# w_out's float64 tiles, from the third on, loaded as two halves into the buffers of the partial results

## The chip, the cores and the metric

One core of one Trainium2 chip. The metric is device time in microseconds (us) of one execution; three executions of the kernel before are shown, and the median is what the prediction is set against.

## What is computed

Three stages in a row, in the precision of float32 results. The weights of the two feed-forward stages are float64; q, k, v and omega are float32.

```python
q_p, k_p = phi(q / D**0.25), phi(k / D**0.25)      # exp(x @ omega.T - |x|^2/2 - max) / sqrt(m)
kv = einsum('bhsm,bhsd->bhmd', k_p, v); z = sum(k_p, axis=2)
x = einsum('bhsm,bhmd->bhsd', q_p, kv) / (einsum('bhsm,bhm->bhs', q_p, z)[..., None] + 1e-06)
x = x.transpose(0, 2, 1, 3).reshape(2304, 512)
y = ((x @ w_a) * (x @ w_b)) @ w_out                # w_a, w_b: 512 x 1536, w_out: 1536 x 512
h = maximum(y @ w_in2, 0); out = (h * h) @ w_out2  # 512 x 2048, 2048 x 512
```

## The kernel before, in words

The change lies in the middle stage, `y = ((x @ w_a) * (x @ w_b)) @ w_out`, which runs interleaved with the attention that makes its `x`.

**Passes.** The hidden width 1536 is cut into 12 tiles f of 128 columns, the 2304 tokens into 9 blocks of 256. `PASSES` (L770) takes block 0 with f = 0 to 5, block 1 with f = 0 to 5, block 0 with f = 6 to 11, block 1 with f = 6 to 11, block 2 in the same two halves, and then pairs of blocks with all f. For each f, `a_units` (L775) issues 24 matmuls "ab" (12 for w_a, 12 for w_b), then, two f later (`LAG`), the 12 matmuls "y" of `outs` (L802), which accumulate over f in the PSUM banks y0 and y1. Every product is three matmuls over a high and a low part of each operand (`TERMS`).

**Weights.** The weights come as float64, 8 bytes a word. `load` (L183) brings them raw into a tile `raw` of [128, 2, 512, 2] int32 (8 KB a partition; the pool has two of them, "the pairs' places"). One `raw` holds either a pair, the tile f of w_a and of w_b (2 x 512 KB), or one tile f of w_out (512 KB, half of the place). `split` (L200) turns the words into float32 high and low parts: ACT scales the upper words (L211), DVE puts sign, exponent and mantissa together in three operations on `p` (L212, L216, L220; the last one reads `raw` and so frees it), ACT casts the high part (L226), DVE subtracts to get the low part (L227). The pairs stay in `W` for good; a tile of w_out goes into one of three `wo` buffers and is stored to `wo_d` (L1603), from which the later passes load it again (L1597). `load_split` (L250) lets at most two loaded tiles wait for their split. Below, o6 to o11 are the tiles f = 6 to 11 of w_out, first needed in the third pass.

**Partial results.** `ypool` has two buffers of [128, 2, 256] float32 (2 KB a partition), tag "ys". They hold `V2` of the attention at the start; `y_s`, the scaled result at the end of a first-half pass, which is stored to `y_d` (L845 to L847); `y_p`, that result loaded again for the second half (`prefetch`, L971), to which DVE adds the new half (L840) and from which it is stored; and, from the seventh pass on, `tz`, weight sums (L889).

**Order.** The code is written in one order, but a scheduler of the Tile framework, with costs of its own, decides how the instructions stand on each engine; each engine and each queue then runs strictly in that order. All loads and stores named here are issued by SP, one after the other: one that waits holds all behind it.

Of the kernel before, what the change touches and what calls it, by code (L numbers as in the profile page):

```python
# [44 lines left out]
def kernel(  # L45
# [13 lines left out]
    nc = tc.nc  # L59
# [121 lines left out]


    def load(*parts):  # L183


        raw = top["raw"].tile([128, 2, 512, 2], I32, tag="raw", name="raw")
        for x, (w, f, rows) in enumerate(parts):
# [12 lines left out]
    def split(raw, t, behind=None, apart=False, put_off=None):  # L200

        n = raw.shape[1]
        a_, p_ = (
            top["cut"].tile([128, 2, 512], F32, tag=x, name=x)[:, 0:n] for x in "ap"
        )
        for x in (slice(0, 1), slice(1, 2)) if apart else (slice(0, n),):
            a, p, r, o = a_[:, x], p_[:, x], raw[:, x], t[:, x]
            with tc.issue_after(behind.ins) if behind else nullcontext():  # L210
                nc.scalar.activation(out=a, in_=f32(r[:, :, :, 1]), func=ACTF.Copy, scale=WORD_SCALE)  # L211
            nc.vector.tensor_scalar(  # L212
# [6 lines left out]
            )  # L219
            nc.vector.scalar_tensor_tensor(  # L220
                out=p.bitcast(U32), in0=r[:, :, :, 0].bitcast(U32), scalar=29,
                in1=p.bitcast(U32), op0=ALU.logical_shift_right, op1=ALU.bitwise_or,
            )

# [550 lines left out]
    def a_units():  # L775
# [26 lines left out]
        def outs(pi, f):  # L802
# [26 lines left out]
            if wide:  # L829
                for c in range(KC):  # L830
                    t = ypool.tile([128, 2, N], F32, tag="ys", name="y_s")
                    nc.scalar.mul(out=t, in_=yp[pi][c], mul=Y_SCALE)
                    for x, i in enumerate(bl):
                        nc.sync.dma_start(out=y_cols(i)[:, c, :], in_=t[:, x, :])
                return
            i = bl[0]
            for c in range(0, KC, 2):
                if f0:
                    t = part[pi, c]
                    nc.vector.scalar_tensor_tensor(  # L840
                        out=t, in0=yp[pi][c // 2], scalar=Y_SCALE, in1=t,
                        op0=ALU.mult, op1=ALU.add,
                    )
                else:
                    t = ypool.tile([128, 2, N], F32, tag="ys", name="y_s")  # L845
                    nc.scalar.mul(out=t, in_=yp[pi][c // 2], mul=Y_SCALE)
# [124 lines left out]
        def prefetch(pi, f):  # L971
            bl, f0, f1 = PASSES[pi]
            if f0 and f == f1 - 1:
                for c in range(0, KC, 2):
                    part[pi, c] = ypool.tile([128, 2, N], F32, tag="ys", name="y_p")
                    nc.sync.dma_start(out=part[pi, c], in_=y_cols(bl[0])[:, c:c + 2, :])
# [813 lines left out]
```

## Time and profile before

| | us |
|---|---|
| three executions | 976.73, 978.43, 978.84 (median 978.43) |
| the profiled execution | 979.28 |
| its span, first to last instruction | 977.2 |
| TensorE (PE) busy | 961.5 (98%) |
| VectorE (DVE) busy | 728.8 (75%) |
| ScalarE (ACT) busy | 551.5 (56%) |
| mean granted TensorE clock | 0.999 of full |

The profile is of one execution. PE is TensorE's matmuls, PEld its weight loads, SPq the queue of loads and stores. A busy share is an average over the whole span; the stages named above lie in its first 310 us, and the third pass (block 0, f = 6 to 11) from about 124 to 174 us.

### The profile page before, as it was taken

To read this page: it belongs to the slowest core of one execution; us is meant where nothing else is said; L and a number is where in the kernel's file an instruction comes from. 1 tells how busy PE (TensorE), PEld (TensorE's weight loads), DVE (VectorE), ACT (ScalarE), POOL (GpSimd) and SP (SyncE) were. 2 spreads that over 40 slices of the span, in tenths; PEclk is the share of its full clock that TensorE was granted. 3 is DMA by queue.
4 is the path that set the end of the run, shared out by engine and by line. 5 is a ranking of instruction groups with operands and counts; after the bars stand their busy time and mean duration, and the time that the engine had idled before them with its cause. 6 is when DMAs were issued, how large, how long until landed. Compare 5 with 4: busy or idle time off the path is not lost.

```text
span 977.2 us, 18208 instructions
## 1 busy us (share of the span) xinstructions
PE 961.5 (98%) x6625; PEld 898.0 (92%) x6625; DVE 728.8 (75%) x1688; ACT 551.5 (56%) x1310; POOL 28.8 (3%) x54
## 2 busy tenths in 40 slices
PE   7999999999999999999999999999999999999998
PEld 6799998999998889889998888899999999999998
DVE  3888689887787865565456989789787347988794
ACT  5876566666655643253433544677676565555561
POOL 4000100000000000000000000000000000000000
PEclk9999999999999999999999999999999999999999
DMA  8656976655775365346547989246666869944301
GB/s 207 208 176 204 307 234 212 226 179 182 218 213 167 130 199 171 113 153 188 170 143 254 350 304 339 66 160 207 216 227 220 317 250 357 390 135 146 115 17 50
DMA packets 121961, 198.39 MB, mean 203 GB/s; under 512 B 28944, under 2 KB 84752, under 8 KB 119440
## 3 DMA queue, kind: packets, MB, share of 16 engines
q1 hardware_dynamic: 120336, 195.65, 60.5%
q0 software_dynamic: 1536, 1.58, 0.6%
q8 instruction: 53, 0.87, 0.4%
q14 instruction: 36, 0.29, 0.1%
HBM read 136.90 MB, written 60.29 MB: 202 GB/s over the span
## 4 chain that ended last, share of the span: by engine, by line
PE 81%; DVE 7%; DMA 5%; ACT 4%; issue 2%; SPq 0%; DVEq 0%; ACTq 0%
PE y L811 13%; PE abw L786 9%; PE oY L1478 8%; PE pY L1294 7%; PE ab L786 7%; PE oX L1478 5%; PE oW L1478 5%; PE sP L919 5%; PE pW L1294 4%; PE sR L919 3%; PE ps_n L638 3%; PE ps_kv L571 3%; PE ps_p L415 3%; PE ps_p L490 2%; DMA raw<-in_moe_w_b_dram 2%; PE ps_qt L628 2%
## 5 line engine op out<-in xcount | busy, mean ns | idle before, releaser
L786 PE MATMUL abw<-x_all,W 128*128 128x512 f32 x432 | 104.1, 392 | 0.0
L786 PEld LDWEIGHTS abw<-x_all,W 128*128 128x128 f32 x432 | 80.0, 188 | 15.7
L786 PE MATMUL ab<-x_all,W 128*128 128x256 f32 x576 | 84.9, 290 | 0.4 <-ACT W L226 0.4
L786 PEld LDWEIGHTS ab<-x_all,W 128*128 128x128 f32 x576 | 74.0, 189 | 1.7 <-ACT W L226 0.6
L811 PE MATMUL y<-g_mid,wo 128*128 128x512 f32 x288 | 75.1, 401 | 0.0
L811 PE MATMUL y<-gs,wo 128*128 128x256 f32 x432 | 66.5, 290 | 0.0
L811 PEld LDWEIGHTS y<-g_mid,wo 128*128 128x128 f32 x288 | 51.9, 188 | 10.1
L811 PEld LDWEIGHTS y<-gs,wo 128*128 128x128 f32 x432 | 56.6, 189 | 1.0 <-DVE wo L227 0.2
L1294 PE MATMUL pY<-W,M 128*128 128x384 f32 x228 | 44.1, 336 | 0.4 <-ACT F L1312 0.4
L499 ACT COPY c<-ps_p 128x256 f32<-128x256 f32 x76 | 27.7, 372 | 28.6 <-PE ps_p L490 28.1
L501 DVE CUSTOM_DVE_ANT_0 c<-ps_p,c 128x128 f32<-128x128 f32 x152 | 38.2, 285 | 7.5 <-ACT c L499 6.8
L786 PE MATMUL ab<-x,W 128*128 128x256 f32 x288 | 42.5, 288 | 0.0
L1442 ACT CAST W<-F 128x384 fp32r<-128x384 f32 x57 | 29.1, 513 | 22.9 <-PE oX L1478 11.0
L1478 PE MATMUL oX<-W 128*128 128x256 f32 x351 | 41.9, 276 | 0.0
L1478 PEld LDWEIGHTS oX<-W 128*128 128x128 f32 x351 | 40.8, 188 | 0.0
L1294 PEld LDWEIGHTS pY<-W,M 128*128 128x128 f32 x228 | 39.8, 188 | 1.0 <-ACT F L1312 0.9
L1320 ACT ACTIVATE F<-F 128x384 f32<-128x384 f32 x48 | 24.7, 518 | 26.9 <-DVE F L1315 26.7
L1478 PE MATMUL oY<-W 128*128 128x256 f32 x315 | 38.6, 277 | 0.0
L786 PEld LDWEIGHTS ab<-x,W 128*128 128x128 f32 x288 | 37.6, 191 | 0.1
L506 ACT ACTIVATE qp<-c,nm 128x128 f32<-128x128 f32 x88 | 31.0, 397 | 11.3 <-DVE nm L501 10.8
L1478 PEld LDWEIGHTS oY<-W 128*128 128x128 f32 x315 | 37.1, 188 | 0.0
L419 DVE TENSOR_REDUCE nm<-ps_p 128x4 f32<-128x512 f32 (+1 forms) x44 | 24.7, 564 | 14.9 <-PE ps_p L415 14.7
(287 smaller groups left out, 2408.7 us busy)
## 6 DMA issues: line engine op xcount, KB each, us to landing
wo<-wo_d SPq DMA_DIRECT2D x60, 512.0 KB, 3.9
s_d<-F SPq DMA_DIRECT2D x24, 768.0 KB, 4.7
tsum<-t_d SPq DMA_DIRECT2D x26, 512.0 KB, 4.0
t_d<-cut SPq DMA_DIRECT2D x40, 256.0 KB, 2.9
raw<-in_moe_w_out_dram SPq DMA_DIRECT2D x32, 256.0 KB, 5.2
raw<-in_moe_w_in_dram SPq DMA_DIRECT2D x16, 512.0 KB, 6.4
raw<-in_moe_w_a_dram SPq DMA_DIRECT2D x12, 512.0 KB, 3.8
raw<-in_moe_w_b_dram SPq DMA_DIRECT2D x12, 512.0 KB, 5.8
```

Source lines behind the costliest of these rows:

```text
L415: state["proj"] = nc.tensor.matmul(ps[:, 2 * x:2 * x + 2].rearrange("p h m -> p (h m)"), lhsT=s, rhs=OMZ.rearrange("p h m -> p (h m)"), st ...
L499: nc.scalar.copy(out=c, in_=ps[:, :, 1, :])
L501: nc.vector.tensor_tensor_reduce(out=c[:, x, :], in0=ps[:, x, 0, :], in1=c[:, x, :], scale=1.0, scalar=3.0e38, op0=ALU.add, op1=ALU.min, a ...
L506: nc.scalar.activation(out=dst[:, 2 * n + x, :], in_=c[:, x, :], func=ACTF.Exp, scale=-1.0, bias=nm[:, x:x + 1],)
L571: lambda h=h, j=j: nc.tensor.matmul(ps[:, h, :], lhsT=kp[:, 4 * h + j, :], rhs=V2[h][:, j] if odd else V[:, j, h, :], start=(j == j0), sto ...
L638: lambda x=x: nc.tensor.matmul(pn[:, x, :], lhsT=t["qT"][:, x % 2 * len(g) + x // 2, :], rhs=kv[:, x % 2, :], start=True, stop=True,)
L786: nc.tensor.matmul(ps, lhsT=wv[:, s_, kc, :], rhs=x[..., kc, m_, :], start=(kc == 0 and (s_, m_) == TERMS[0]), stop=(kc == KC - 1 and (s_, ...
L811: nc.tensor.matmul(y_part(pi, f, c), lhsT=wo[pi, f][:, s_, c * 128:(c + 1) * 128], rhs=g[:, m_, :],  start=(f == f0 and (wide or c % 2 == ...
L919: nc.tensor.matmul(ps[:, z], lhsT=b(z, s_, kk), rhs=a[:, kk, m_, :], start=(first and z == 0 and kk == 0 and (s_, m_) == TERMS[0]), stop=( ...
L1294: nc.tensor.matmul(ps[c][:, x, 0:TH], lhsT=w[:, s_, 128 * kk:128 * kk + 128], rhs=y[:, ai, kk, m_, :], start=((c, x) not in seen and kk == ...
L1442: ahead_of["cast"] = nc.scalar.copy(out=sop[:, 0], in_=src)
L1478: nc.tensor.matmul(tiles_of(p, t), lhsT=sops[n][:, s_, 128 * t:128 * t + 128], rhs=w[:, m_, :], start=(fresh and k == 0 and (t % 2 == 0 or ...
```

## The change

The tiles of w_out with f >= 2 no longer go into `raw`. Each is loaded as two halves of 512 int32 columns (256 KB, 2 KB a partition) into two buffers of `ypool`. `split` then reads the halves apart: two ACT operations in place of one for the upper words, two DVE operations in place of one for the last step on `p`; the other steps stay whole. `y_stage` allocates the partial results' buffers, and first has all waiting w_out tiles of that kind split.

```diff
--- before.py
+++ after.py
@@ -180,9 +180,27 @@
 
 
 
+    O_APART = 2
+
+    def y_stage(name):
+
+        while any(x[1][0] == "o" and x[1][1] >= O_APART for x in waiting):
+            split_next()
+        return ypool.tile([128, 2, N], F32, tag="ys", name=name)
+
     def load(*parts):
 
 
+        if parts[0][2] and parts[0][1] >= O_APART:
+            w, f, _ = parts[0]
+            raws = []
+            for z in range(2):
+                t = ypool.tile([128, 2, N], F32, tag="ys", name="rawo").rearrange("p a n -> p (a n)")
+                nc.sync.dma_start(
+                    out=i32(t), in_=w[f * 128:(f + 1) * 128, 512 * z:512 * z + 512]
+                )
+                raws.append(i32(t).rearrange("p (f w) -> p f w", w=2))
+            return raws
         raw = top["raw"].tile([128, 2, 512, 2], I32, tag="raw", name="raw")
         for x, (w, f, rows) in enumerate(parts):
             t = raw[:, x]
@@ -201,14 +219,24 @@
 
 
 
-        n = raw.shape[1]
+        halves = None
+        if isinstance(raw, list):
+            halves = [(slice(256 * z, 256 * z + 256), r) for z, r in enumerate(raw)]
+        n = 1 if halves else raw.shape[1]
         a_, p_ = (
             top["cut"].tile([128, 2, 512], F32, tag=x, name=x)[:, 0:n] for x in "ap"
         )
         for x in (slice(0, 1), slice(1, 2)) if apart else (slice(0, n),):
-            a, p, r, o = a_[:, x], p_[:, x], raw[:, x], t[:, x]
+            a, p, o = a_[:, x], p_[:, x], t[:, x]
+            if halves:
+                pieces = [(a[:, 0, c], p[:, 0, c], r) for c, r in halves]
+            else:
+                pieces = [(a, p, raw[:, x])]
             with tc.issue_after(behind.ins) if behind else nullcontext():
-                nc.scalar.activation(out=a, in_=f32(r[:, :, :, 1]), func=ACTF.Copy, scale=WORD_SCALE)
+                for a_x, _, r in pieces:
+                    nc.scalar.activation(
+                        out=a_x, in_=f32(r[..., 1]), func=ACTF.Copy, scale=WORD_SCALE
+                    )
             nc.vector.tensor_scalar(
                 out=i32(p), in0=i32(a), scalar1=3, scalar2=0x7FFFFFF8,
                 op0=ALU.logical_shift_left, op1=ALU.bitwise_and,
@@ -217,10 +245,11 @@
                 out=i32(p), in0=i32(a), scalar=-0x80000000, in1=i32(p),
                 op0=ALU.bitwise_and, op1=ALU.bitwise_or,
             )
-            nc.vector.scalar_tensor_tensor(
-                out=p.bitcast(U32), in0=r[:, :, :, 0].bitcast(U32), scalar=29,
-                in1=p.bitcast(U32), op0=ALU.logical_shift_right, op1=ALU.bitwise_or,
-            )
+            for _, p_x, r in pieces:
+                nc.vector.scalar_tensor_tensor(
+                    out=p_x.bitcast(U32), in0=r[..., 0].bitcast(U32), scalar=29,
+                    in1=p_x.bitcast(U32), op0=ALU.logical_shift_right, op1=ALU.bitwise_or,
+                )
 
             def parts(o=o, p=p):
                 state["cast"] = nc.scalar.copy(out=o[:, :, 0, :], in_=p)
@@ -828,7 +857,7 @@
                 return
             if wide:
                 for c in range(KC):
-                    t = ypool.tile([128, 2, N], F32, tag="ys", name="y_s")
+                    t = y_stage("y_s")
                     nc.scalar.mul(out=t, in_=yp[pi][c], mul=Y_SCALE)
                     for x, i in enumerate(bl):
                         nc.sync.dma_start(out=y_cols(i)[:, c, :], in_=t[:, x, :])
@@ -842,7 +871,7 @@
                         op0=ALU.mult, op1=ALU.add,
                     )
                 else:
-                    t = ypool.tile([128, 2, N], F32, tag="ys", name="y_s")
+                    t = y_stage("y_s")
                     nc.scalar.mul(out=t, in_=yp[pi][c // 2], mul=Y_SCALE)
                 nc.sync.dma_start(out=y_cols(i)[:, c:c + 2, :], in_=t)
 
@@ -972,7 +1001,7 @@
             bl, f0, f1 = PASSES[pi]
             if f0 and f == f1 - 1:
                 for c in range(0, KC, 2):
-                    part[pi, c] = ypool.tile([128, 2, N], F32, tag="ys", name="y_p")
+                    part[pi, c] = y_stage("y_p")
                     nc.sync.dma_start(out=part[pi, c], in_=y_cols(bl[0])[:, c:c + 2, :])
 
         t_now = {}
```

The numbers of matmuls, of casts and of stores stay; ten loads, ten ACT and ten DVE operations are added. Since the scheduler goes by other load times, it also sets the instructions anew: PE's order is another one between its 184th and its 1713th matmul of 6271, and the same again from there on. Three pieces follow, as the built programs have them; changed line numbers are those of the changed file, which are 29 higher from L226 on.

The first is from SP's queue, at the end of the second pass. `raw` and `rawo` are loads of float64 words, `wo_d` are stores of finished tiles of w_out (92 is o6), `y_s` the partial result. Before:

```order
L190 DMA raw<-in_moe_w_out_dram 128x1024
L441 DMA qn<-in_q_dram 128x2x64
L194 DMA raw<-in_moe_w_a_dram 128x4x256
L1603 DMA wo_d_92<-wo 128x1024
L194 DMA raw<-in_moe_w_b_dram 128x4x256
L847 DMA y_d_103<-y_s 128x2x256 x2
L1603 DMA wo_d_93<-wo 128x1024
L190 DMA raw<-in_moe_w_out_dram 128x1024
L976 DMA y_p<-y_d_103 128x2x256 x2
L194 DMA raw<-in_moe_w_a_dram 128x4x256
L194 DMA raw<-in_moe_w_b_dram 128x4x256
```

and now:

```order
L212 DMA raw<-in_moe_w_a_dram 128x4x256
L212 DMA raw<-in_moe_w_b_dram 128x4x256
L470 DMA qn<-in_q_dram 128x2x64
L199 DMA rawo<-in_moe_w_out_dram 128x512 x2
L1632 DMA wo_d_92<-wo 128x1024
L470 DMA qn<-in_q_dram 128x2x128
L876 DMA y_d_103<-y_s 128x2x256
L1632 DMA wo_d_93<-wo 128x1024
L876 DMA y_d_103<-y_s 128x2x256
L199 DMA rawo<-in_moe_w_out_dram 128x512
L470 DMA qn<-in_q_dram 128x2x128
L199 DMA rawo<-in_moe_w_out_dram 128x512 x3
```

The last pair (f = 11) stood behind the load of o8 and stands now ahead of that of o7; the loads of y_p are gone from here, and those of o8 stand behind the stores of y_s, whose buffers they take.

The second is from SP's queue, at the end of the third pass (`wo<-wo_d_92` loads o6 again for the fourth). Before:

```order
L190 DMA raw<-in_moe_w_out_dram 128x1024
L1603 DMA wo_d_95<-wo 128x1024
L441 DMA kn<-in_k_dram 128x2x256
L1603 DMA wo_d_96<-wo 128x1024
L1597 DMA wo<-wo_d_92 128x1024
L1603 DMA wo_d_97<-wo 128x1024
L1597 DMA wo<-wo_d_93 128x1024
L847 DMA y_d_103<-y_p 128x2x256 x2
```

and now:

```order
L199 DMA rawo<-in_moe_w_out_dram 128x512 x2
L1632 DMA wo_d_96<-wo 128x1024
L1005 DMA y_p<-y_d_103 128x2x256 x2
L1626 DMA wo<-wo_d_92 128x1024
L1632 DMA wo_d_97<-wo 128x1024
L1626 DMA wo<-wo_d_93 128x1024
L876 DMA y_d_103<-y_p 128x2x256 x2
```

The loads of y_p now stand behind the load of o11, whose buffers they take, and ahead of the first load for the fourth pass.

The third is from PE, at the end of the third pass (y_1895 and y_1896, now y_1921 and y_1922) and the begin of the fourth's sums (y_2496, now y_2536). Before:

```order
L786 MATMUL ab<-x_all,W 128x256 x13
L490 MATMUL ps_p<-OM,S 128x256 x2
L786 MATMUL ab<-x_all,W 128x256
L811 MATMUL y_1895<-gs,wo 128x256 x2
L811 MATMUL y_1896<-gs,wo 128x256 x2
L786 MATMUL ab<-x_all,W 128x256
L811 MATMUL y_1895<-gs,wo 128x256 x4
L811 MATMUL y_1896<-gs,wo 128x256 x4
L628 MATMUL ps_qt<-ident,qp 128x128 x4
L786 MATMUL ab<-x_all,W 128x256 x10
L811 MATMUL y_2496<-gs,wo 128x256 x6
```

and now:

```order
L815 MATMUL ab<-x_all,W 128x256 x18
L840 MATMUL y_1921<-gs,wo 128x256 x2
L840 MATMUL y_1922<-gs,wo 128x256 x2
L444 MATMUL ps_p<-OMZ,T 128x256
L840 MATMUL y_1921<-gs,wo 128x256 x3
L680 MATMUL ps_x<-ident,xh 128x128 x2
L840 MATMUL y_1921<-gs,wo 128x256
L840 MATMUL y_1922<-gs,wo 128x256 x4
L519 MATMUL ps_p<-OM,S 128x256 x2
L815 MATMUL ab<-x_all,W 128x256 x5
L494 MATMUL ps_t_2482<-ident,qn 128x128 x2
L815 MATMUL ab<-x_all,W 128x256 x5
L840 MATMUL y_2536<-gs,wo 128x256 x6
```

The y matmuls of o11 begin as the 1060th matmul of the order and began as the 1026th; those of the fourth pass begin as the 1089th, not the 1053rd, 15 after the last of o11. Those of o9 begin as the 955th (before: 953rd), and from the 1166th on the fourth pass stands where it stood.

## Rows read from the trace of the kernel before

**Rows 1.** The page, busy time: engine, us (share of the span), instructions.
```profile
PE 961.5 (98%) x6625; PEld 898.0 (92%) x6625; DVE 728.8 (75%) x1688; ACT 551.5 (56%) x1310; POOL 28.8 (3%) x54
```

**Rows 2.** Who PE waited for, 113 to 310 us: us in total, times, longest us.
```profile
PE ps_qt L628 <- ACT qp L506: 0.7, 1, 0.7
PE ps_qt L628 <- DVE nm L501: 0.7, 1, 0.7
PE ps_nt L694 <- ACT qT L690: 0.4, 2, 0.2
PE ab L786 <- ACT W L226: 0.4, 1, 0.4
PE ps_qt L628 <- ACT qp L421: 0.3, 1, 0.3
PE ps_xt L706 <- DVE xh L613: 0.2, 1, 0.2
```

**Rows 3.** Who SP's queue waited for, whole span: us in total, times, longest us.
```profile
SPq L190 <- DVE p L220: 27.0, 9, 5.7
...
SPq L194 <- DVE p L220: 18.6, 9, 4.5
```

**Rows 4.** Busy time of each engine (instructions), clock, DMA share, GB/s, 155 to 180 us.
```profile
155.00:180.00 25.00, 24.13 (x193) 22.68 (x193) 23.51 (x70) 15.89 (x41) 1.04 (x2) 1.00 0.65 211
```

**Rows 5.** Groups of DVE, then ACT, by shape, 113 to 180 us: busy us, mean ns.
```profile
L220 DVE SCALAR_TENSOR_TENSOR p<-raw,p 128x512 uint32<-128x512 uint32 x8 | 5.5, 686 | 0.1
...
L1064 DVE TENSOR_TENSOR a_s<-ab,a_s 128x256 f32<-128x256 f32 x11 | 4.6, 420 | 1.0 <-ACT a_s L1063 1.0
...
L211 ACT ACTIVATE a<-raw 128x512 f32<-128x512 f32 x8 | 5.4, 676 | 4.8 <-DVE den L609 1.6 <-DMA raw<-in_moe_w_b_dram 1.4 <-DVE den L612 1.0
...
L1063 ACT ACTIVATE a_s<-ab 128x256 f32<-128x256 f32 x11 | 4.1, 382 | 6.5 <-PE ab L786 6.5
```

**Rows 6.** DMA issues, 113 to 180 us: KB each, median us from issue to landing.
```profile
raw<-in_moe_w_out_dram SPq DMA_DIRECT2D x6, 512.0 KB, 3.8
...
raw<-in_moe_w_a_dram SPq DMA_DIRECT2D x3, 512.0 KB, 3.6
...
y_d<-y_s SPq DMA_DIRECT2D x2, 256.0 KB, 6.3
y_p<-y_d SPq DMA_DIRECT2D x2, 256.0 KB, 3.9
```

**Rows 7.** SP's queue in order of time: start us, us to issue, what.
```profile
137.17 1.44 SPq L847 DMA_DIRECT2D y_d<-y_s  x2
...
143.69 0.93 SPq L976 DMA_DIRECT2D y_p<-y_d  x2
...
161.87 0.33 SPq L190 DMA_DIRECT2D raw<-in_moe_w_out_dram  x1
...
168.97 0.37 SPq L1597 DMA_DIRECT2D wo<-wo_d  x1
```

**Rows 8.** PE in order of time, third pass: start us, us, what [idle before].
```profile
159.52 2.84 PE L786 MATMUL ab<-x_all,W 128*128 128x256 f32 x22
...
162.51 0.74 PE L811 MATMUL y<-gs,wo 128*128 128x256 f32 x4
...
172.22 0.66 PE L811 MATMUL y<-gs,wo 128*128 128x256 f32 x4
...
175.52 0.87 PE L811 MATMUL y<-gs,wo 128*128 128x256 f32 x6
```

**Rows 9.** ACT in order of time: the split of o11.
```profile
165.45 0.67 ACT L211 ACTIVATE a<-raw 128x512 f32<-128x512 f32 x1
...
171.46 0.62 ACT L226 CAST wo<-p 128x512 fp32r<-128x512 f32 x1 [0.20 <-DVE p L220]
```

**Rows 10.** DVE in order of time: the split of o11, then the sum.
```profile
170.74 0.69 DVE L220 SCALAR_TENSOR_TENSOR p<-raw,p 128x512 uint32<-128x512 uint32 x1
...
173.64 1.29 DVE L840 SCALAR_TENSOR_TENSOR y_p<-y,y_p 128x512 f32<-128x512 f32 x2
```

## The prediction, as put on record before the run

> **What bounds the kernel now.** I read the page's busy times first: PE is busy 98% of the span [rows 1]. A change that adds no matmul and takes none away can therefore gain only what PE waits. The change reorders PE's work from its 184th to its 1713th matmul and no further, so I asked next for whom PE waited in that part: from 113 to 310 us it is 2.7 us in all (0.7 + 0.7 + 0.4 + 0.4 + 0.3 + 0.2), and of these only 0.4 us is a wait for the weights, the cast W at L226; the rest are transposes and small products of the attention that wait for ACT or DVE [rows 2]. SP's queue, asked for its own waits, shows what the change goes for: loads of w_out stood 27.0 us in total, and loads of pairs 18.6 us, until DVE had read a raw place [rows 3]. So the places are short, but nearly all of that shortage is hidden: PE had other matmuls in its order. Last, the stretch from 155 to 180 us: DVE is busy 23.51 of 25 us, ACT 15.89, PE 24.13 [rows 4]. There DVE, not the loads, is the engine with least room, and there the last four tiles of w_out are split.
>
> About 0.2%, here 2 us, is what a measurement of this kernel can tell from no change. All waits of rows 2 together are little more than that.
>
> **The change, part by part.** Removed: the turns that pairs and w_out's tiles take at the two raw places. In the first order piece the last pair (f = 11) moves from behind the load of o8 to ahead of that of o7. That pair is the one whose cast PE waits for at about 157.7 us. Gain taken: 0.4 us, that one wait [rows 2]. Bounds: nothing, if DVE is as late with the pair's low part as the load was; 1.3 us, if the waits of the attention in the same stretch (0.4 + 0.3 + 0.2) go too because ACT and DVE are less held up in front of a load.
>
> Added on DVE and ACT: ten times two half operations in place of one. A DVE operation of 256 columns takes 0.420 us, the whole step of 512 takes 0.686 us, so a split costs 2 x 0.420 - 0.686 = 0.15 us, ten of them 1.5 us; on ACT it is 2 x 0.382 - 0.676 = 0.09 us, ten of them 0.9 us [rows 5]. (The 256-column rows are of other operations on float32, the nearest shown.) ACT's share is hidden: it is free for 9 us of the 25 us of the fullest stretch [rows 4]. On DVE four of the ten lie between 155 and 180 us, 4 x 0.15 = 0.6 us, with 1.5 us of room. Taken: +0.3 us, half; bounds 0 and +0.6.
>
> Added on SP: ten more issues of 0.33 us or so [rows 7], 3.3 us spread over 110 us; SP spends far more than that waiting [rows 3], and that wait is the cover. Where SP does not wait for a free place but for a landing, there is no cover: that is the next point.
>
> A half brings half the bytes, but no earlier landing is counted: y_p, 256 KB, lands 3.9 us after issue, w_out, 512 KB, 3.8 [rows 6]. The pieces don't matter either in these rows: w_a comes in pieces of 1 KB (256 words of 4 bytes, L195) and lands in 3.6 us, w_out in rows of 4 KB [rows 6]. The Trainium skill (Perfetto Trace Analysis, DMA Optimizations) speaks against the halves: small transfers, under 2 KB, carry much overhead each, and going from 2 to 4 or 8 KB can help throughput much; these halves go from 4 KB a partition to 2. By that rule each half would land later than the whole did, and the slower rival below would be the likelier; the 1 KB pieces of w_a show no such loss, so I keep 3.9 us.
>
> **The wait that the change adds.** The two buffers of the partial results now hold one tile of w_out at a time. Four tiles in a row (o8 to o11) and then y_p pass through the same two buffers, each load behind the last read of the one before. What one turn takes at least: landing 3.9, second issue 0.3, an ACT half 0.38, the three DVE steps 0.42 + 0.69 + 2 x 0.42 = 1.95; together 6.5 us [rows 5, 6, 7]. Before, with two raw places, the next load ran beside the split: o11 was issued at 161.87 us and its split began on ACT at 165.45 [rows 7, 9]. What PE's order allows for a turn: between the first y of o9 and the first y of o11 there stood 73 matmuls, in 172.22 - 162.51 = 9.71 us, 0.133 each [rows 8]; now 105 stand there, so 14.0 us for two turns, 7.0 each. So a turn fits with half a microsecond to spare, if the split is done at once. It was not always: o11's split took from 165.45 to the start of its last step at 170.74, 5.3 us where the operations alone need 1.8 (0.67 + 0.42 + 0.69), because both engines work in order [rows 5, 9, 10]. Lower bound of the cost: 0. Upper: two turns each late by 6.5 + 3.5 - 7.0 = 3.0 us, 6 us. Taken: 0, since before, too, o11's cast ended at 172.08 and its y began at 172.22 without a wait [rows 8, 9], that is, PE's order had been made to meet the splits closely and it held.
>
> Then y_p. Before, it was loaded at 143.69 us and used at 173.64, 30 us later [rows 7, 10]; a late one cost nothing. Now its loads stand behind the last reads of o11 (second order piece). From the end of o11's last step: y_p lands after 0.4 + 3.9 = 4.3 us [rows 6, 7], the first of two sums of 0.64 us (1.29 for both) is done at 5.0 [rows 10]. PE needs the bank that this sum frees for the first y of the fourth pass. From the same point PE begins the y of o11 after the cast, 0.6 to 0.7 us [rows 9], and reaches the fourth pass's y 29 matmuls later (1060th to 1089th, third order piece), 29 x 0.13 = 3.8 us, at 4.5 us. So 0.5 us of PE time is missing; +0.5 us, with 0 (if o11 is split ahead of its y) and 2 us (a landing like y_s's 6.3 [rows 6]) as bounds. Queued behind y_p on SP is the load of o6 for the fourth pass, which goes out as late; before it went at 168.97 us for a y at 175.52 [rows 7, 8], 6.5 us ahead, so it has some 2 us in hand over a landing.
>
> The partial result's own stores (y_s, 6.3 us to landing [rows 6], issued at 137.17 [rows 7]) now hold up the load of o8, to about 144 us; before, y_p's loads waited there just so, until 143.69. No cost is taken, as o8's y stands 12 matmuls later than it did.
>
> After the 1713th matmul the order is the old one, and what comes after 310 us moves as a block.
>
> Sum: -0.4 + 0.3 + 0 + 0.5 = +0.4 us. The profiled execution, 979.28 us, would become 979.7; it stands 0.85 us over the median of the runs, 978.43, and against that median the forecast is 978.8 us.
>
> **The rivals.** *Slower: the turns at the two buffers set the pace.* The place is the third pass, o9 to y_p; it decides as soon as a turn takes more than 7.0 us. For it: DVE has 1.5 us of room in 25 [rows 4], and o11's split took 3.5 us over its bare operations. Against: the order met the splits within 0.2 us before. Price: o10 and o11 each late by 1 to 1.5 us and y_p's 0.5 to 2 on top: +2.5 to +5, less the 0.4 gained: 980.5 to 983.0 us. Chance 0.3. *Faster: the pairs' earlier loads free the small engines.* ACT stood 1.4 us before loads of pairs in its 512-column operations alone, between 113 and 180 us [rows 5], and the attention's products wait on ACT and DVE [rows 2]. If that clears three quarters or more of the 2.7 us of rows 2, and the turns keep up: 975.7 to 976.4 us. For it is that the waits at 18.6 us of SP's queue fall on pairs [rows 3]; against it that the two longest waits, 0.7 each, lie after the third pass and have to do with no load of weights. Chance 0.2. *No change to speak of because nothing that mattered was moved:* the pairs land earlier and PE's order still has the same matmuls, so 978.0 to 979.0 us; it lies within the forecast's case.
>
> **How the numbers follow.** Forecast's case (within 2 us of 978.4, its own range 977.0 to 980.3) 0.5, slower 0.3, faster 0.2; these are the three chances as well. The range takes all of the forecast's case, the slower one up to 982.4 and the upper part of the faster one from 976.1: 976.1 to 982.4.
>
> **What would show it.** Right: PE's wait for W at L226 is gone; SP's waits of w_out's loads are no shorter, those of pairs are; y_p is issued past 170 us and its sum on DVE waits for a DMA; a y of the fourth pass, or its weight load, begins with a wait of about 0.5 us for that sum. Wrong towards slower: PE idle before y for wo (L255, L256) at o10 or o11, summing to 2 us or more. Wrong towards faster: rows 2's waits mostly gone, with y_p landed before the y of o11 ends.

## The result, and the profile after

The changed kernel takes 984.78 us (median of 6 executions, 982.59 to 986.43); the kernel before, beside it, 978.19 (6 executions, 975.95 to 979.28). Ratio 1.0071, 95% interval 1.0054 to 1.0087: 6.6 us slower, outside the range that was given. The profiled execution has a span of 983.6 us, against 977.2.

The page, busy time (as [rows 1]):

```profile
PE 963.7 (98%) x6625; PEld 897.2 (91%) x6625; DVE 729.9 (74%) x1698; ACT 553.9 (56%) x1320; POOL 29.0 (3%) x54
```

PE's busy time rose by 2.2 us with the same number of matmuls, so most of the loss is idle time. Who PE waited for, 113 to 317 us (us in total, times, longest; as [rows 2]):

```profile
PE y L840 <- DMA wo<-wo_d: 1.2, 1, 1.2
PE ps_xt L735 <- DVE xh L642: 0.9, 1, 0.9
PE ps_qt L657 <- DVE nm L530: 0.7, 1, 0.7
PE ps_p L444 <- ACT T L434: 0.6, 1, 0.6
PE ps_nt L723 <- ACT qT L719: 0.4, 1, 0.4
PE ps_p L519 <- DVE x_all L689: 0.4, 1, 0.4
```

The wait for the cast W is gone. In its place stands one of 1.2 us for a reload of w_out's tile o6, and more waits of the attention's small products for DVE and ACT than before. What SP's queue waited for (as [rows 3]):

```profile
SPq L199 <- DVE p L249: 26.7, 8, 5.3
...
SPq L212 <- DVE p L249: 22.6, 7, 7.1
```

w_out's loads wait as long for a place as they did (27.0 us), the pairs' longer (18.6 before). The stretch from 155 to 180 us (as [rows 4]):

```profile
155.00:180.00 25.00, 23.25 (x181) 21.37 (x180) 21.53 (x64) 14.09 (x39) 0.00 (x0) 1.00 0.43 152
```

DVE, called there the engine with least room, is less busy than before (23.51), and the DMA engines' share fell from 0.65 to 0.43: of w_out's tiles each is now loaded only when the one before is split, as the next rows show.

**The turns.** SP's queue in order of time (start, us to issue, what), third pass:

```profile
144.81 0.34 SPq L199 DMA_DIRECT2D rawo<-in_moe_w_out_dram  x1
...
163.38 0.80 SPq L199 DMA_DIRECT2D rawo<-in_moe_w_out_dram  x2
...
170.93 0.81 SPq L199 DMA_DIRECT2D rawo<-in_moe_w_out_dram  x2
...
177.34 0.89 SPq L1005 DMA_DIRECT2D y_p<-y_d  x2
178.32 0.43 SPq L1626 DMA_DIRECT2D wo<-wo_d  x1
```

These are the first half of o8, then o10, o11, y_p, and the reload of o6. DVE in order of time shows what frees the places:

```profile
157.04 1.22 DVE L249 SCALAR_TENSOR_TENSOR p<-raw,p 128x1024 uint32<-128x1024 uint32 x1
158.18 0.28 DVE L642 TENSOR_TENSOR xh<-ps_nt,den 64x128 f32<-64x128 f32 x1
...
159.72 1.23 DVE L256 TENSOR_TENSOR W<-p,W 128x1024 fp32r<-128x1024 f32 x1 [0.56 <-ACT W L255]
...
162.88 0.76 DVE L249 SCALAR_TENSOR_TENSOR p<-rawo,p 128x256 uint32<-128x256 uint32 x2
...
170.44 0.76 DVE L249 SCALAR_TENSOR_TENSOR p<-rawo,p 128x256 uint32<-128x256 uint32 x2
...
176.85 0.76 DVE L249 SCALAR_TENSOR_TENSOR p<-rawo,p 128x256 uint32<-128x256 uint32 x2
```

The last reads of o9, o10 and o11 begin at 162.88, 170.44 and 176.85: turns of 7.6 and 6.4 us, and o9's own took 10.7 (o8's last read began at 152.22), since DVE did the pair's two steps at 157.04 and 159.72 first. And PE:

```profile
159.21 0.33 PE L735 MATMUL ps_xt<-ident,xh 128*128 128x128 f32 x1 [0.87 <-DVE xh L642]
...
164.35 0.74 PE L840 MATMUL y<-gs,wo 128*128 128x256 f32 x4
...
172.20 0.67 PE L840 MATMUL y<-gs,wo 128*128 128x256 f32 x4
...
178.98 0.62 PE L840 MATMUL y<-gs,wo 128*128 128x256 f32 x4
...
184.07 1.04 PE L840 MATMUL y<-gs,wo 128*128 128x256 f32 x7 [1.18 <-DMA wo<-wo_d]
```

The first y of o9, o10 and o11 begin without a wait, though 1.8, 5.0 and 6.8 us later than before: PE had `ab` matmuls in front of them. The waits are elsewhere: for xh, which DVE did behind the pair's split, and before the fourth pass's first y.

**Where the loss lies.** Both traces have 6625 matmul records. For each kernel I took the start of the 400th, 700th, 950th, 1350th, 1500th and 2200th record (counted from 0), less the same in the kernel before (about 68, 106, 138, 190, 209 and 299 us there). The differences give what a stretch lost (us). The first two columns are the median of the kernel against that of the kernel before in the same session, and the last is how many of PE's 720 places from the 1380th to the 2100th matmul hold another operation than in the kernel before / in the changed one, by the built programs (6271 matmuls for 6625 records, so a place and a record have different numbers):

```
                 median   +us   first pass  third pass  4th-5th pass   order there
                                400 to 700  950 to 1350 1500 to 2200   before/after
after            984.78  +6.6     +1.8        +3.0         +2.8         84 /  0
third_only       984.51  +5.9      0.0        +5.0         +2.4         84 /  0
first_only       981.73  +3.1     +1.7        +1.0         +1.3          8 / 83
halves_in_raw    978.40  -0.2     +0.6        +1.3         +0.1        138 /151
odd_apart        978.83  +0.2     +0.1        +1.1         +0.6        132 /148
even_apart       979.33  +1.0     +1.1        -0.6         +1.3        156 /161
yp_in_raw        984.10  +5.7     +1.7        +3.4         +3.8         84 /  8
turns_alone      982.61  +4.3      0.0        +2.4         +4.9         84 /  8
odd_yp_in_raw    982.53  +4.2      0.0        +0.7         +3.9         84 /  8
last2            982.33  +3.5      0.0        +3.3         +0.8         10 / 82
last3            986.08  +7.2     +0.1        +3.6         +2.4         76 / 23
four_apart       980.94  +2.1      0.0        +2.5         +1.5          8 / 83
five_apart       984.30  +5.4      0.0        +3.7         +2.9         91 / 34
order_only       982.19  +3.0      0.0         0.0         +4.3         84 /  8
yp_reversed      984.31  +5.1     +1.6        +2.5         +2.9        168 / 86
all_but_o2       984.73  +5.5     +0.5        +2.7         +3.9         84 /  0
all_but_o11      983.75  +4.5     +1.6        +3.0         +2.2         12 / 80
```

The stretches come from one profiled execution each, the medians from 4 to 11; a stretch is read to about half a microsecond. The rows below `after` are the experiments.

The columns do not add up to the whole, for two reasons. The two longest waits of [rows 2], 0.65 us each, lie just outside them, at 197.11 and 301.19 us of the kernel before; where another order has no such wait, that time comes back. The changed kernel is without the first of them and gets back 0.8 us between the 1350th and the 1500th record; order_only is without both, and its 4.3 us in the stretch are 3.0 us in all. And in five of the profiled executions, third_only, yp_in_raw, last2, last3 and five_apart, the granted clock fell once within the third pass. By the windows, as worked out for last2 below, that is 1.7 us of each of these five figures, and they are the five highest of the column.

### The profile page after: what moved, and what is told of

The parts are those of the page before. It is cut to its first block, busy times and chain, and to the rows that moved or that the text cites. A ratio compares the mean times of both kernels' runs of the same rounds, so it can differ in the third digit from the quotient of the medians.

```text
span 983.6 us, 18238 instructions
## 1 busy us (share of the span) xinstructions
PE 963.7 (98%) x6625; PEld 897.2 (91%) x6625; DVE 729.9 (74%) x1698; ACT 553.9 (56%) x1320; POOL 29.0 (3%) x54
## 4 chain that ended last, share of the span: by engine, by line
PE 81%; DVE 7%; DMA 6%; ACT 4%; issue 2%; SPq 0%; DVEq 0%; ACTq 0%
PE y L840 14%; PE abw L815 10%; PE oY L1507 7%; PE pY L1323 7%; PE ab L815 7%; PE oX L1507 5%; PE sP L948 5%; PE oW L1507 4%; PE pW L1323 4%; PE sR L948 3%; PE ps_n L667 3%; PE ps_p L444 3%; DMA t_d<-cut 2%; PE ps_kv L600 2%; PE ps_p L519 2%; PE ps_qt L657 2%
## 5 line engine op out<-in xcount | busy, mean ns | idle before, releaser
L519 PE MATMUL ps_p<-OM,S 128*128 128x256 f32 x152 | 33.9, 306 | 1.9 <-DVE x_all L689 0.4
```

The lines of the kernel that those rows point to most:

```text
L519: lambda ps=ps, o_=o_, x=x: nc.tensor.matmul(ps[:, x].rearrange("p a m -> p (a m)"), lhsT=self.s[:, x, o_:o_ + 128], rhs=OM.rearrange("p a ...
```

## Experiments

Where `O_APART` is changed it is made a set (`>= O_APART` becomes `in O_APART`), so that one can choose which tiles of w_out go through the two buffers. The diffs are excerpts. Theories: **T**, a tile that can be loaded only when the tile before it is split costs time (turns). **Y**, the partial results behind the turns, y_p and the reload of o6 behind it, cost. **O**, the order that the scheduler makes of later work costs, whatever goes through the buffers. **B**, the split operations on DVE cost. The first four expectations say **A** for T and Y together, and **C** for the first form of O: that any new order costs.

**Which tiles, and is it the halves?** Four kernels of one session.

```diff
-    O_APART = 2
+    O_APART = set(range(6, 12))      # third_only
+    O_APART = set(range(2, 6))       # first_only
+    O_APART = {3, 5, 7, 9, 11}       # odd_apart
```

```diff
 # halves_in_raw: all ten tiles in halves, in the pairs' places
+            whole = top["raw"].tile([128, 2, 512, 2], I32, tag="raw", name="raw")
             for z in range(2):
-                t = ypool.tile([128, 2, N], F32, tag="ys", name="rawo").rearrange("p a n -> p (a n)")
+                t = whole[:, 0, 256 * z:256 * z + 256]
```

Expected of third_only:

> Only o6 to o11 go in halves into the partial results' buffers; o2 to o5 go whole into the raw places as before. Theory A (the turns at the two buffers, and y_p behind them, make PE late): the loss of the third pass stays, about 3 us by the two traces, and that of the first pass (about 1.5 us) goes: +3 to +5 us over the kernel before, ratio 1.003 to 1.005. Theory B (the split operations on a nearly full DVE): 6 of 10 splits remain, +4 us spread over the splits, with no long wait of w_out's loads. Theory C (any new order of the scheduler costs): no rule, as much as the whole change, +6.6.

Expected of first_only:

> Only o2 to o5 go apart; o6 to o11 go whole into the raw places, y_p is loaded early again. Theory A: the first pass's loss alone, +1 to +2 us over the kernel before, and no late y_p. Theory B: 4 of 10 splits, +2.6 us. Theory C: as much as the whole change, +6.6.

Expected of halves_in_raw:

> All ten tiles are loaded and split in halves, but both halves lie in a raw place as before, so the partial results keep their buffers to themselves. Theory A: nothing lost, within 1 us of the kernel before. Theory B: the whole +6.6 us, since all the added operations and loads are there. Theory C: something between, for the order is another one here too.

Expected of odd_apart:

> Only the odd tiles from f = 3 on go apart in halves, the even ones go whole into a raw place, so that the load of one tile runs beside the split of the one before. Theory A: turns no longer follow one another in one place; most of the loss goes, but y_p still stands behind o11: 0 to +2.5 us. Theory B: 5 of 10 splits, +3.3 us. Theory C: as much as the whole change.

Measured, as ratios: third_only 1.0061 (1.0046 to 1.0076), first_only 1.0030 (1.0018 to 1.0043), halves_in_raw 0.9999 (0.9989 to 1.0008), odd_apart 1.0007 (0.9994 to 1.0020). B falls: ten loads, ten ACT and ten DVE operations more cost nothing that can be told (the interval is -1.1 to +0.8 us). Every other tile in the buffers costs nothing to speak of (at most 2 us by the interval). C falls with them: both have an order further from the old one than the changed kernel's (138 and 132 places against 84) and lose next to nothing. The two parts do not add up, 5.9 + 3.1 is more than 6.6, and both came out above what A expected, so something besides the turns may be at work.

**y_p, or the turns themselves?** y_p of the third and fourth pass goes into a pairs' place, and stands on SP's queue ahead of the reload and of o10 or o11.

```diff
 # yp_in_raw; odd_yp_in_raw with O_APART = {3, 5, 7, 9, 11};
 # turns_alone with set(range(6, 12)), and y_s of the second pass likewise in a pairs' place
+                if pi in (2, 3):
+                    whole = f32(top["raw"].tile([128, 2, 512, 2], I32, tag="raw", name="y_p"))
                 for c in range(0, KC, 2):
-                    part[pi, c] = y_stage("y_p")
+                    if pi in (2, 3):
+                        part[pi, c] = whole[:, c // 2].rearrange("p f w -> p (f w)")[:, 0:2 * N].rearrange("p (a n) -> p a n", a=2)
+                    else:
+                        part[pi, c] = y_stage("y_p")
```

even_apart is the changed kernel with `O_APART = {2, 4, 6, 8, 10}`. Expected of yp_in_raw:

> The changed kernel, all ten tiles in turns, but y_p of the third and the fourth pass is loaded into a pairs' place, so it stands on SP ahead of o10, not behind the last read of o11, and the reload of o6 (wo<-wo_d) behind it goes out earlier. Theory Y (the late y_p and the reload behind it are a part of the loss): PE's 1.2 us wait of the fourth pass's first y for wo_d is gone, +4.5 to +5.5 us over the kernel before instead of +6.6. Theory T (the turns themselves and what they do to the order cost it all, y_p only waits in their shadow): the time stays within 0.7 us of the changed kernel's, +6 to +7.

Expected of turns_alone:

> Only o6 to o11 in turns, y_s of the second pass and y_p of the third and fourth in the pairs' places, so that nothing but tiles of w_out goes through the two buffers in the third pass. Against third_only (+5.9) this takes away the 0.9 us wait of y for y_s and the 1.0 us wait for the reload. Theory Y: +3.5 to +4.5 us remain. Theory T: +5.5 to +6.5. If nearly nothing remains (under +1.5), the tiles' own turns fit and all of the loss was y_s and y_p, the partial results.

Expected of odd_yp_in_raw:

> Only o3, o5, o7, o9, o11 in turns, and y_p of the third and fourth pass in a pairs' place. odd_apart showed no loss (+0.2) but PE still waited 0.6 us for the reload of o6 behind y_p. Theory Y: 0.3 to 0.7 us below odd_apart, so -0.4 us against the kernel before, 977.7 to 978.4. Theory T: as odd_apart, within 0.5 us of the kernel before. Either way it is hardly to be told from no change; a gain over 1.5 us would say that the pairs' places were worth more than PE's waits show.

Expected of even_apart:

> o2, o4, o6, o8, o10 in turns, the others in the pairs' places. If it is the back-to-back turns that cost (one tile's load can only go out when the tile before is split), the loss is gone as in odd_apart: -1 to +1.5 us. If a single tile's turn or the place it takes from y_s (before o8) costs, +1 to +3 us, since here o8 stands right behind y_s.

Measured: yp_in_raw 1.0061 (1.0044 to 1.0078), turns_alone 1.0040 (1.0026 to 1.0055), odd_yp_in_raw 1.0043 (1.0029 to 1.0056), even_apart 1.0011 (1.0002 to 1.0020). In yp_in_raw the wait for the reload is gone, and the time is not: PE waits elsewhere in the same stretch (PE in order of time):

```profile
160.96 0.33 PE L735 MATMUL ps_xt<-ident,xh 128*128 128x128 f32 x1 [1.61 <-DVE xh L642]
```

The granted clock was 0.77 and 0.89 in the windows of 160 to 165 and 165 to 170 us. So in this execution the 1.2 us were lost again in another place. It was the slowest of the four (986.84 us); their median, +5.7 us, lies between what Y and T expected, and its interval overlaps that of the changed kernel. Whether Y is worth up to a microsecond there is not shown. turns_alone, +4.3, lies in Y's range, but only 2.4 us of it in the third pass and 4.9 behind it; even_apart came out within its first range. The surprise is odd_yp_in_raw: 4 us where nothing was expected. Its third pass lost 0.7 us; 3.9 us went between 209 and 299 us, in work that the edit hardly touches. There PE's order was the changed kernel's but for 8 places. Theory O in its later form, that this order costs, comes from this run.

**Turns against order.** Among sets of tiles I chose four whose PE order in the fourth and fifth pass is the old one (last2, four_apart) or close to the changed kernel's (last3, five_apart).

```diff
-    O_APART = 2
+    O_APART = {10, 11}               # last2
+    O_APART = {9, 10, 11}            # last3
+    O_APART = {6, 7, 9, 11}          # four_apart
+    O_APART = {6, 8, 9, 10, 11}      # five_apart
```

Expected of last2:

> Only o10 and o11 in turns, one behind the other, then y_p. PE's order in the fourth and fifth pass is the old one but for 10 places of 720. Theory T (each load that must wait for the split of the tile before costs, in the third pass): one such turn, +0.3 to +1.5 us up to 190 us, nothing after it; in all 0 to +1.5. Theory O (a second loss sits in the order that the scheduler makes of the fourth and fifth pass, and comes with that order, not with turns): under +0.7 us between 190 and 350 us.

Expected of last3:

> o9, o10 and o11 in turns: one tile more than last2, but PE's order in the fourth and fifth pass is now nearly the changed kernel's (23 places of 720 differ from it, 76 from the kernel before). Theory T: two turns behind one another, +0.6 to +2.5 us in the third pass, nothing after 190 us. Theory O: on top of it +1.5 to +3 us between 190 and 350 us; in all +2.5 to +5.

Expected of four_apart:

> o6, o7, o9 and o11 in turns; o7 behind o6 and o11's load behind nothing but o9's split long before. PE's order after the third pass is the kernel before's but for 8 places of 720. Theory T: one turn (o7 behind o6) and o9 behind y_s, +0 to +1.5 us in all. Theory O: nothing between 190 and 350 us (under +0.7). If it costs +3 or more, neither holds and any use of the two buffers by w_out costs.

Expected of five_apart:

> o6 and o8 to o11 in turns, o7 in a pairs' place. Four tiles in a row go through the two buffers as in the changed kernel, and PE's order of the fourth and fifth pass is close to the changed kernel's (34 places of 720 differ from it, 91 from the kernel before). Theory T: +2 to +4 us in the third pass, as in the changed kernel and third_only. Theory O: +1.5 to +3 us more between 190 and 350 us; in all +4 to +6.5. If the stretch after 190 us shows under +0.7, O falls.

Measured: last2 1.0044 (1.0026 to 1.0062), last3 1.0076 (1.0063 to 1.0089), four_apart 1.0022 (1.0013 to 1.0031), five_apart 1.0054 (1.0042 to 1.0067). By stretch O holds roughly: 0.8 and 1.5 us with the old order, 2.4 and 2.9 with the other, though 0.8 and 1.5 are more than the 0.7 that O allowed. All four lost 2.5 us or more in the third pass, above what T allowed for all but five_apart. The profiled execution of last2 shows where, first on PE, then in the windows of 5 us around it (busy us and count of PE, PEld, DVE, ACT, POOL, then PE's granted clock, DMA share, GB/s):

```profile
177.82 1.26 PE L840 MATMUL y<-gs,wo 128*128 128x256 f32 x5 [1.94 <-DMA wo<-wo_d]
```

```profile
170.00:175.00 5.00, 5.00 (x46) 5.00 (x44) 4.97 (x17) 3.13 (x9) 0.00 (x0) 1.00 0.56 132
175.00:180.00 5.00, 3.06 (x17) 2.70 (x17) 1.51 (x8) 1.18 (x3) 0.00 (x0) 0.80 0.97 365
180.00:185.00 5.00, 5.00 (x37) 4.78 (x36) 3.63 (x13) 3.19 (x10) 0.00 (x0) 0.86 0.81 243
```

Two turns and y_p behind them put the reload of o6 late; PE waited 1.94 us, and its granted clock, at 1.00 before, was 0.80 and 0.86 of full in the two windows (a part of each at the lower of its two levels, 1.2 in place of 2.4 GHz), which is worth 5 x (0.20 + 0.14) = 1.7 us more: 3.6 us, about the whole loss of last2's third pass (3.3). In this execution Y is the cost. Three others of its seven had a mean clock of 1.000, so no such fall (it takes 0.0017 off the mean), and took 981.88 to 983.95 us against 981.31 for this one; what they lost instead is not shown.

**The order alone.** Since the cause was still open, four more.

```diff
 # order_only: the kernel BEFORE, y_p of the fourth pass alone in a pairs' place
+                if pi == 3:
+                    whole = f32(top["raw"].tile([128, 2, 512, 2], I32, tag="raw", name="y_p"))
                 for c in range(0, KC, 2):
-                    part[pi, c] = ypool.tile([128, 2, N], F32, tag="ys", name="y_p")
+                    if pi == 3:
+                        part[pi, c] = whole[:, c // 2].rearrange("p f w -> p (f w)")[:, 0:2 * N].rearrange("p (a n) -> p a n", a=2)
+                    else:
+                        part[pi, c] = ypool.tile([128, 2, N], F32, tag="ys", name="y_p")
 # yp_reversed: the changed kernel, y_p's second half loaded first
-                for c in range(0, KC, 2):
+                for c in range(KC - 2, -1, -2):
                     part[pi, c] = y_stage("y_p")
 # all_but_o2, all_but_o11
+    O_APART = {3, 4, 5, 6, 7, 8, 9, 10, 11}
+    O_APART = {2, 3, 4, 5, 6, 7, 8, 9, 10}
```

Expected of order_only:

> The kernel before, all tiles of w_out in the pairs' places, none in halves; only y_p of the fourth pass goes into a pairs' place. That gives PE, from its 1380th matmul on, the changed kernel's order but for 8 places (84 differ from the kernel before). Theory O (the loss between the 1500th and the 2200th recorded matmul comes with that order, whatever goes through the two buffers): +2 to +4 us in that stretch, under +1 in the third pass, in all +2 to +4.5. If turns, halves or the delay of the third pass are what costs there: under +1 in that stretch and within 1.5 us of the kernel before in all.

Expected of yp_reversed:

> The changed kernel, but the two loads of each y_p are issued in the other order (second half first). PE's order is the changed kernel's up to its 1380th matmul and another from there to the 2100th (86 places differ from the changed kernel, 168 from the kernel before). Theory O: first pass +1.5 to +2 and third pass +3 to +4 as in the changed kernel (the first sum of y_p now waits for the second load, up to 0.5 us more), and the stretch of the 1500th to 2200th matmul moves by 1 us or more, down or up, from the changed kernel's +2.8. If it stays at +2.8 within 0.5 us, the order there is not what costs.

Expected of all_but_o2:

> The changed kernel with o2 in a pairs' place, o3 to o11 in turns. PE's order of the first 700 matmuls is then nearly the kernel before's (35 places differ, against 158), all after it the changed kernel's. Theory O: the first pass loses nothing (under +0.6, where the changed kernel loses 1.8), the rest stays: +4 to +5.5 us in all. Theory T (turns cost in the first pass too): o3 to o5 still take three turns one behind the other, so +1.2 to +1.8 stays there, +6 to +7 in all.

Expected of all_but_o11:

> The changed kernel with o11 in a pairs' place, so y_p stands behind o10's split, not o11's; five tiles (o6 to o10) still go one behind the other. PE's order from the 1380th matmul on is the kernel before's but for 12 places. Theory O: under +1.3 us in the stretch of the 1500th to 2200th matmul. Theory Y (in the third pass it is the late reload of o6, and the lower clock after that wait, that costs): third pass under +1.5, in all +2 to +4 with the first pass's 1.8. Theory T (the row of turns costs): third pass +2 to +3.5, in all +4 to +6.

Measured: order_only 1.0031 (1.0017 to 1.0045), yp_reversed 1.0053 (1.0037 to 1.0069), all_but_o2 1.0054 (1.0037 to 1.0071), all_but_o11 1.0046 (1.0029 to 1.0063).

order_only has no tile of w_out in the two buffers and no halves, loses nothing in the first and the third pass, and 4.3 us between 209 and 299 us. One row of busy time for 209 to 285 us, in the kernel before, the changed kernel and order_only (columns as above):

```profile
209.00:285.00 76.00, 75.56 (x627) 73.28 (x627) 61.06 (x233) 50.43 (x157) 3.50 (x6) 1.00 0.67 202
```

```profile
209.00:285.00 76.00, 74.16 (x601) 70.53 (x601) 61.38 (x228) 50.47 (x155) 3.50 (x6) 1.00 0.65 205
```

```profile
209.00:285.00 76.00, 74.22 (x595) 69.99 (x594) 56.88 (x218) 49.23 (x153) 3.51 (x6) 1.00 0.60 185
```

627 matmuls in that window before, 601 and 595 after: 26 fewer at 76/627 = 0.121 us each are 3.1 us. Of this 1.4 us is idle time of PE, 1.8 us in place of 0.4; by the view of waits it is for the attention's small products, and the longest are 0.4 us in the changed kernel and 0.7 in order_only. The rest is no idle time in the rows; there the matmuls follow one another at a longer mean distance, and why is not shown. This loss is the order's, not that of turns, halves or a late third pass: last2's third pass is late by 3.3 us and it loses 0.8 there. Nor is it the place that y_p takes in order_only: its loads went out at 166.04 us (before: 181.43), and the last load of weights into a pairs' place at 161.57. The order is here that of DVE, ACT and SP's queue as well, which the scheduler set anew together with PE's. And it is not just any other order: halves_in_raw and odd_apart have other orders and lost 0.1 and 0.6 there. yp_reversed missed: a third order, 86 places from the changed kernel's, loses just as much (+2.9), so the loss is not bound to one exact order. Nor is the old order safe: all_but_o11 has it but for 12 places and lost 2.2, against under 1.3 expected.

all_but_o2 takes the turns out of question in the first pass: o3 to o5 still take theirs, and the loss there is 0.5 us, not 1.8. The row of 68 to 106 us in all_but_o2, then in the changed kernel:

```profile
68.00:106.00 38.00, 37.95 (x297) 36.12 (x296) 31.98 (x74) 25.16 (x69) 4.66 (x8) 1.00 0.61 202
```

```profile
68.00:106.00 38.00, 36.68 (x286) 34.78 (x285) 32.42 (x71) 24.52 (x65) 4.77 (x8) 1.00 0.60 200
```

So it comes with moving o2, not with turns; every kernel with o2 in the two buffers lost 1.1 to 1.8 us there, every other one 0.6 or less. That it is the order, and not the place of o2, PE's rows show. First the changed kernel, then the kernel before:

```profile
75.46 0.71 PE L723 MATMUL ps_nt<-kvr,qT 128*128 128x130 f32 x4 [0.41 <-ACT qT L719]
...
82.05 0.38 PE L494 MATMUL ps_t<-ident,kn 128*128 128x128 f32 x2
83.10 0.70 PE L444 MATMUL ps_p<-OMZ,S 128*128 128x256 f32 x2 [0.68 <-ACT S L497]
```

```profile
83.70 0.60 PE L465 MATMUL ps_t<-ident,kn 128*128 128x128 f32 x4
84.06 1.42 PE L786 MATMUL ab<-x_all,W 128*128 128x256 f32 x10
...
85.79 0.60 PE L415 MATMUL ps_p<-OMZ,S 128*128 128x256 f32 x2
```

ACT copies the transposes ps_t to S, which takes it 0.59 us, and the product ps_p reads S. Before, 13 matmuls stood between the two and hid the copy; now ps_p stands right behind ps_t, and PE waits 0.68 us. No load and no tile of w_out is in this wait. All six kernels with o2 in the buffers have these two waits, 0.41 and 0.67 to 0.68 us, and the eleven others have neither: 1.1 of the 1.8 us. In total all_but_o2 gained nothing by it, since its fourth and fifth pass lost 3.9 us, 1.1 more than the changed kernel's with the same order of PE. all_but_o11 shows the third pass without any wait for the reload, and it still loses 3.0 us: in that stretch it is not Y alone. Its waits there are for xh, W and qT, so it is T or again the order.

No kernel of these is faster than the kernel before.

## Why the prediction was wrong

**The sum had no term for the new order.** "After the 1713th matmul the order is the old one, and what comes after 310 us moves as a block" is true within a microsecond, but only the third pass was priced, and the reordered part runs from the first pass on. It lost 1.8 us in the first pass and 2.8 between 209 and 299 us, 4.6 us in all. "The change reorders PE's work" was read off and then used only to choose where to look for waits, and even that from 113 us on, behind the first pass. order_only shows that such an order costs about 3 us by itself (1.7 to 4.4 by the interval); in the first pass two waits of the attention's products, 1.1 us, come straight from places in the new order.

**"Taken: 0" for the turns** is the second failed step: the third pass lost 3.0 us. "What one turn takes at least", 6.5 us, was nearly met by the last one (6.4), but o9's took 10.7, as DVE had the pair's split first. The transfer was not what made them long: a landing was taken as 3.9 us and measured 2.9 (median, 113 to 190 us).

```profile
rawo<-in_moe_w_out_dram SPq DMA_DIRECT2D x10, 256.0 KB, 2.9
```

The bound above it, 6 us, held. In the table the six kernels in which no tile of the third pass is loaded behind the split of the tile next before it lost -0.6 to +1.3 us there; the eleven in which one is, 2.4 to 5.0, or 1.6 to 3.3 without the 1.7 us of the lower clock in five of them, so the two groups lie close. The wait that would be the turn itself, y for the cast of w_out's tile, sums to 1.4 us in four_apart, 1.0 in five_apart and 0.8 in turns_alone, and is not there in the changed kernel. What is waiting for the turn, and what the order made around it, is not separated: here the cause stays open.

**The sign named for it was useless.** "PE idle before y for wo at o10 or o11, summing to 2 us or more" did not show: the first y of each begins within 0.2 us of its cast without a wait. By that sign the kernel would not have been slower. The scheduler had put other work ahead of y, and the loss came out as waits of the attention and for the reload: [rows 2]'s view sums to 2.7 us before and, over all its eleven rows of after, to 5.7. Two signs of being right did not show either: the pairs' loads waited longer, not shorter, and the fourth pass's first y waited for the reload, not for the sum.

**y_p, +0.5 us.** y_p did issue past 170 us (177.34), and its second sum waited 0.36 us for it. The fourth pass's first y waited 1.2 us, but for the reload of o6 queued behind y_p, which "has some 2 us in hand over a landing". It went out at 178.32 us, 5.7 us before that y, and landed after 5.6; the slack was sized by the 3.8 us of another transfer of this size [rows 6]. Taken alone the term's bound of 2 us was too low as well: in the profiled execution of last2 the same wait cost 3.6 us with the clock.

**What held.** PE's wait for W is gone, and buys nothing that can be seen. The halves are about as sized: 0.42 us on DVE, and on ACT 0.43 where 0.38 was taken. By groups and shape, DVE, then ACT, 113 to 190 us:

```profile
L249 DVE SCALAR_TENSOR_TENSOR p<-rawo,p 128x256 uint32<-128x256 uint32 x12 | 4.5, 420 | 0.1
```

```profile
L237 ACT ACTIVATE a<-rawo 128x256 f32<-128x256 f32 x12 | 5.0, 433 | 3.4 <-DVE den L641 2.1 <-DMA rawo<-in_moe_w_out_dram 0.8 <-DVE p L244 0.6
```

The +0.3 us taken for them is not to be told from nothing (halves_in_raw, -0.2). The rule of the Trainium skill (Perfetto Trace Analysis, DMA Optimizations) on small transfers, that batching them from 2 KB to 4 or 8 KB can improve throughput much, is one on throughput. It does not say that a half lands later, as the prediction had it; here a half landed after 2.9 us where a whole took 3.8 [rows 6], and going from 4 KB a partition to 2 KB cost no time, as the 1 KB pieces of w_a in the trace of before had suggested (w_b's, of the same size and queued right behind them, landed after 5.4 us there, which the prediction left out).

**The rivals.** The slower one had the right side and half of the right place; its 980.5 to 983.0 us missed by 1.8 us because it, too, priced the third pass alone, and the waits at o10 and o11 that it was made of did not show. The faster one rested on [rows 2]'s waits clearing; they grew.

## What to carry to other kernels

Where a scheduler sets the order, an edit of buffers is also an edit of the order of everything behind it. Compare the orders before predicting and look where a product has come to stand right behind the copy that it reads, as ps_p behind S did. Give each reordered stretch its own term, with zero as one bound and not as the value, and test it by an edit that gives the same order without the change, as order_only did. A place that holds one tile at a time turns load, landing and split into one chain; alternate it with another place (odd_apart cost nothing that could be told) or leave it alone.

## What was not expected of the hardware

The granted clock. After the wait of 1.94 us it fell in last2, as shown; in third_only waits of 0.90 and 0.47 us before 160 us were followed by a window at 0.66 (160 to 165 us), while the changed kernel, with 0.87 and 0.44 us at the same place, stayed at 1.00. The window in third_only:

```profile
160.00:165.00 5.00, 5.00 (x33) 5.00 (x32) 3.97 (x12) 1.00 (x3) 0.00 (x0) 0.66 0.31 96
```

The same wait can cost its own length or about 1.7 us more (5 x 0.34), and the length of the wait alone does not tell which: PE also waited 1.34 us in turns_alone (150.35) without a fall.
